# A decode attention kernel: K and V in three pieces per head in place of four, and w_o earlier in the last head

## The chip, the cores and the metric

One core of a Trainium2 chip, the others idle. The metric is the device time of one execution in microseconds. "Span" is what the profile shows between the first and the last instruction; the time is mostly 1.3 to 1.7 us longer, now and then up to 2.9 us, so spans are the steadier number and are given where they decide.

## The reference, cut to what matters

```
x: 1 x 512 (one token), 32 query heads, 8 K/V heads, 65536 cached tokens, head size 128, bf16
q = layernorm(x) @ wq
for each K/V head h:                       # K[h], V[h]: 65536 x 128, 16 MB each
    p = softmax(q[4h:4h+4] @ K[h].T * 128**-0.5)
    o[4h:4h+4] = p @ V[h]
h  = x + o @ wo                            # wo: 4096 x 512, 4 MB
h2 = h + (sigmoid(g) * u) @ w_down         # g, u = layernorm(h) @ w_gate, w_up; 1.75 MB each
```

Nearly everything is the reading of 268 MB of K and V, once.

## The kernel before

SBUF holds a ring of four slots of 32 KB per partition. A load of K or V is 4 MB: 128 rows of 32 KB, 16384 tokens, four loads per head for each of K and V. A slot is split in 8 "chunks" of 4 KB per partition. All loads go through one queue, in order; each waits until its slot is free:

```python
order = [("wq", 0)] + [("K", b) for b in range(NR)]          # NR = 4 loads per head
for b in range(NR, NB):                                       # NB = 32
    order += [("K", b), ("V", b - NR)]
order += [("V", NB - 4), ("V", NB - 3), ("V", NB - 2), ("V", NB - 1), ("wg", 0), ("wu", 0), ("wd", 0)]
# ... slot = position % 4; a load waits for the user of its slot: F{b} (K transposed) or PV{b} (V used)
src = cache[0, h, r * BLK:(r + 1) * BLK, :].rearrange("(p t) d -> p (t d)", t=T)
dma("sp", lambda e, d=dst, sr=src: e.dma_start(d, sr), ..., deps, f"{k}{b}")
if ld == ("V", NB - 4):                                       # w_o follows the last head's first V load
    for i, (j0, nj) in enumerate(WO):                         # WO = ((0, 28), (28, 4)) rows
        dma("sp", ..., f"wo{i}", [f"G{HKV - 1}"] if i == 0 else (), f"wo{i}")
```

DVE transposes K's chunks into a second buffer (8 chunks), PE multiplies them with q (scores), DVE and ACT do the softmax, DVE transposes the probabilities, PE multiplies them with V: "rounds" of 8 matmuls on two chunks of V. The last V load comes in two parts (3 MB and 1 MB). PE's program is one loop over heads with branches for what differs:

```python
if v == NB - 3:                 # last head, after its first V load's rounds
    project7()                  # 28 rows of w_o against the 7 finished heads: one row of 512
...
if v == NB - 1:                 # last head, in front of the last V load's rounds
    columns()                   # that row turned into 4 columns: 4 small fp32 matmuls
op("pe", lambda e: None, [f"V{v}" if v < NB - 1 else f"V{v}.0"] + ...)   # wait for V
pv(v)                           # rounds; before the last one a wait for the last part of V
```

After the last round: output of the head, the last 4 rows of w_o, layernorm, w_gate and w_up, tanh, w_down.

## Time and profile before

| | before |
|---|---|
| time, median of 3 runs | 658.38 us (658.36 to 658.48) |
| span of the profiled run | 657.1 us |
| DMA engines busy | 99.7% of the span |
| PE, DVE busy | 64%, 53% |
| one head's period (eight 4 MB loads) | 77.45 us, 433.2 GB/s |

The prediction below shows the lines. Read them in this order: the engine that is never idle (DMA), then the period of the steady part against its bytes, then who waits at the end. DVE's bracket "[10.27 <-DMA ...]" says that it sat idle for 10.27 us until K arrived: the computing engines follow the stream, they don't lead it.

### The profile page before, as it was taken

The numbers are of one execution on the slowest core, as the hardware profiler recorded it, in microseconds if no ns is written. First come the engines' busy times: TensorE is split into PE (matmuls) and PEld (weight loads), VectorE is DVE, ScalarE is ACT, GpSimd is POOL, SyncE is SP. The second block draws the span as 40 slices with busy tenths as digits, with TensorE's granted clock in tenths as the row PEclk, the third lists the DMA queues.
The fourth block names the chain that finished last, engine by engine and source line by source line (L and its number), as shares of the span: only waits on it lengthen the run. The fifth ranks groups of instructions, "written<-read, shape, count | busy, mean of one in ns | idle before, by whom it ended". The sixth has DMA issues, their size and how long they took to land. (4 is left out here: it accounts for less than half of the span.)

```text
span 657.1 us, 6111 instructions
## 1 busy us (share of the span) xinstructions
PE 420.5 (64%) x2315; PEld 74.1 (11%) x1547; DVE 349.7 (53%) x439; ACT 42.9 (7%) x114; POOL 3.6 (1%) x17
## 2 busy tenths in 40 slices
PE   0688488548666585576765575764866668556746
PEld 0200011011000010010100110101100001001322
DVE  2399775547537665347555374465743575542202
ACT  1100200020000200020000200002000100002001
POOL 1000000000000000000000000000000000000000
PEclk9989689677888697776966769765888869677676
DMA  9999999999999999999999999999999999999998
GB/s 383 447 433 429 439 423 431 431 447 415 447 415 447 437 425 447 415 447 419 443 441 421 447 415 447 423 439 443 419 447 415 447 427 435 445 417 427 435 430 352
DMA packets 10802, 282.34 MB, mean 430 GB/s; under 512 B 1329, under 2 KB 1330, under 8 KB 1842
## 3 DMA queue, kind: packets, MB, share of 16 engines
q1 hardware_dynamic: 10658, 282.33, 99.7%
q10 hardware_dynamic: 144, 0.00, 0.0%
HBM read 282.33 MB, written 0.00 MB: 430 GB/s over the span
## 5 line engine op out<-in xcount | busy, mean ns | idle before, releaser
L431 PE MATMUL PS<-ktw 128*128 128x512 bf16 x1024 | 299.9, 442 | 157.4 <-DVE ktw L511 153.6
L511 DVE STREAM_TRANSPOSE ktw<-ring 128x1024 f32<-128x1024 f32 x256 | 291.6, 1205 | 128.0 <-DMA ring<-in_A_k_cache_dram 128.0
L431 PE MATMUL PS<-ring,PT_sb 128*32 x1024 | 83.9, 455 | 23.6 <-issue 13.2
L431 PEld LDWEIGHTS PS<-ktw 128*128 x256 | 27.1, 106 | 408.2 <-issue 256.8
L565 DVE STREAM_TRANSPOSE PT_sb<-P_sb 128x512 bf16<-128x512 bf16 x32 | 20.2, 684 | 54.0 <-PE PS L602 52.3
L551 ACT ACTIVATE negmax<-PS 128x1 f32<-128x1 f32 x8 | 1.4, 171 | 520.6 <-PE PS L549 520.6
L431 PEld LDWEIGHTS PS<-ring,PT_sb 128*32 x1024 | 25.8, 116 | 79.8 <-issue 74.6
L516 DVE TENSOR_REDUCE M_sb<-PS 128x1 f32<-128x512 f32 x32 | 19.9, 684 | 25.5 <-PE PS L431 25.5
L555 ACT ACTIVATE P_sb<-PS,negmax 128x512 bf16<-128x512 f32 x32 | 21.6, 686 | 0.3
L572 DVE TENSOR_REDUCE lsum<-PS 128x1 f32<-128x4 f32 x8 | 1.3, 163 | 31.2 <-PE PS L570 31.2
L542 PE MATMUL PS<-identf,gm 128*1 128x128 f32 x16 | 3.4, 301 | 16.9 <-DVE gm L540 16.9
L616 DVE TENSOR_TENSOR Lw<-O,blk_of 128x896 bf16<-128x896 bf16 (+1 forms) x2 | 1.4, 683 | 20.6 <-ACT O L606 20.6
L402 PE MATMUL PS<-st,onesf 128*128 128x2 f32 x4 | 1.2, 362 | 16.1 <-DVE st L401 16.1
L431 PE MATMUL PS<-ring,xz 128*8 x32 | 9.2, 459 | 2.3 <-issue 2.3
L599 ACT ACTIVATE po_sb<-PS,rl 128x512 bf16<-128x512 f32 x8 | 5.5, 687 | 53.2 <-PE PS L431 53.2
L431 PE MATMUL PS<-ktw,O 128*1 x26 | 7.6, 464 | 0.0
L549 PE MATMUL PS<-one_f,gmrep 1*128 1x1 f32 x16 | 4.2, 330 | 5.0 <-DVE gmrep L546 5.0
L555 ACT ACTIVATION_READ_ACCUMULATOR P_sb<-PS,negmax 128x1 f32 x32 | 6.5, 202 | 0.0
L476 DVE STREAM_TRANSPOSE qt<-qh 32x512 bf16<-32x512 bf16 x1 | 0.7, 699 | 10.6 <-ACT qh L473 10.6
L602 PE MATMUL PS<-sel_bf,po_sb 128*128 128x4 bf16 x32 | 2.0, 168 | 6.4 <-ACT po_sb L599 6.4
L417 DVE CAST hT<-x_col 128x4 f32<-128x4 bf16 x1 | 0.2, 171 | 10.6 <-DMA x_col<-in_A_x_dram 10.6
L661 DVE COPY yr<-PS 1x512 f32<-1x512 f32 x1 | 0.7, 679 | 8.3 <-PE PS L659 8.3
(82 smaller groups left out, 74.0 us busy)
## 6 DMA issues: line engine op xcount, KB each, us to landing
ring<-in_A_k_cache_dram SPq DMA_DIRECT2D x32, 4096.0 KB, 28.7
ring<-in_A_v_cache_dram SPq DMA_DIRECT2D x31, 4096.0 KB, 26.4
ring<-in_A_wq_dram SPq DMA_DIRECT2D x1, 4096.0 KB, 12.3
ktw<-in_A_wo_dram SPq DMA_DIRECT2D x1, 3584.0 KB, 12.7
ring<-in_A_v_cache_dram SPq DMA_DIRECT2D x1, 3072.0 KB, 13.2
ring<-in_B_w_gate_dram SPq DMA_DIRECT2D x1, 1792.0 KB, 19.0
ring<-in_B_w_up_dram SPq DMA_DIRECT2D x1, 1344.0 KB, 21.7
ring<-in_A_v_cache_dram SPq DMA_DIRECT2D x1, 1024.0 KB, 15.2
```

The source lines that it names most:

```text
L431: return e.add_instruction(mybir.InstMatmult(name=nc.get_next_instruction_name(), engine=mybir.EngineType.PE, ins=[rhs, lhsT], outs=[e.low ...
L511: op("dve", lambda e, d=dst, sr=src: e.transpose(d, sr), deps, f"T{b}.{c}", to="T")
L516: op("dve", lambda e, u=u: e.tensor_reduce(M_sb[:, u % 4:u % 4 + 1], ps(u % NS, 0, 512), AX.X, ALU.max), [f"S{b}.{NC - NR + k}"], f"mx{u}" ...
L542: op("pe", lambda e: e.matmul(ps(MISC, 0, 128, 0, 1), lhsT=gm[:, :], rhs=identf[:, :], start=True, stop=True), [f"gm{h}"], f"gmT{h}", to="Q")
L549: op("pe", lambda e: e.matmul(ps(MISC, 128, 129), lhsT=gmrep[0:1, :], rhs=one_f[0:1, 0:1], start=True, stop=True), [f"gmrep{h}"], f"neg{h}")
L551: op("act", lambda e: e.activation(negmax[:, k:k + 1], ps(MISC, 128, 129), AF.Copy, scale=-att_scale), [f"neg{h}"], f"negmax{h}")
L555: op("act", lambda e, b=b: e.activation(P_sb[:, (b % 4) * 512:(b % 4 + 1) * 512], ps(b % NS, 0, 512), AF.Exp, bias=negmax[:, k:k + 1], sca ...
L565: op("dve", lambda e, b=b: e.transpose(PT_sb[:, (b % 4) * 512:(b % 4 + 1) * 512], P_sb[:, (b % 4) * 512:(b % 4 + 1) * 512]), [f"E{b}", f"o ...
L572: op("dve", lambda e: e.tensor_reduce(lsum[:, :], ps(MISC, 132, 136), AX.X, ALU.add), [f"l{h}"], f"ls{h}", to="D")
L599: op("act", lambda e: e.activation(po_sb[:, :], ps(PO, 0, 512), AF.Copy, scale=rl[:, :]), [f"PV{NR * h + NR - 1}", f"rl{h}"], f"po{h}", to ...
L602: op("pe", lambda e, t=t: e.matmul(ps(OX, 0, 4), lhsT=po_sb[:, t * 128:(t + 1) * 128], rhs=sel_bf[:, 8 * t:8 * t + 8:2], start=(t == 0), s ...
L616: op("dve", lambda e: e.tensor_tensor(Lw[i][:, :].rearrange("p (j c) -> p j c", j=n), bass.AP(tensor=O2, offset=j0, ap=[[NQ, 128], [1, n], ...
```

## The change

Its intent: fewer loads on the stream that bounds the kernel, and work out of the tail. A head's K and V come in pieces of 12, 8 and 12 chunks (48, 32, 48 KB per partition; 6, 4, 6 MB). K and V now overlap in the same ring of 32 chunks, and a piece is freed part by part, by marks in the middle of it. V's rounds are regrouped (10 and 6 in place of 4 x 4). In the last head w_o is loaded between V's first and second piece, and the 28 rows and the columns are done after six rounds. V's last part is 2 MB, two rounds.

```diff
-    SLOT = T * DH
+    PIECES = ((0, 12), (12, 20), (20, 32))
+    RING = 32 * CH
+    AT = {"K": (0, 0, 8), "V": (12, 24, 20), "K0": (0, 12, 20), "V7": (0, 12, 20), "wq": 24, "wg": 0, "wd": 7}
...
+        LAST = [(20, 28), (28, 32)]
...
+        for h in range(1, HKV):
+            load("K", h, 0, ["F0.1" if h == 1 else f"F{h - 1}.3"], "ka", f"K{h}.0")
+            load("V", h - 1, 0, ["F0.3" if h == 1 else f"PV{h - 2}.3:2"], "va", f"V{h - 1}.0")
+            load("V", h - 1, 1, ["F0.4" if h == 1 else f"PV{h - 2}.3"], "vb", f"V{h - 1}.1")
+            load("K", h, 1, [f"F{h}.0"], "ka", f"K{h}.1")
+            load("K", h, 2, [f"F{h}.1", f"PV{h - 1}.0:4"], "kb", f"K{h}.2")
+            load("V", h - 1, 2, [f"PV{h - 1}.0"], "vb", f"V{h - 1}.2")
+        h = HKV - 1
+        load("V", h, 0, [f"F{h}.3"], "va", f"V{h}.0")
+        for i, (j0, nj) in enumerate(WO):
...
+            dma("sp", ..., f"wo{i}", [f"PV{h - 1}.3"] if i == 0 else (), f"wo{i}")
+        load("V", h, 1, (), "vm", f"V{h}.1")
+        for i, cols in enumerate(LAST):
+            load("V", h, 2, (), ("vb", "vl")[i], f"V{h}.2{('', 'b')[i]}", cols)
...
-            op("dve", lambda e: e.memset(scr[:, b:b + 1], 0.0), (), f"F{b}")
+                mark = {7: 0, 11: 1, 23: 3}.get(j, 4 if h == 0 and j == 31 else None)
...
-                for p in ("A0", "B0", "A1", "A2", "A3", "A4"):
+                for p in ("A0", "A4", "B0", "A1", "A2", "A3"):
...
+                    if last:
+                        pv(i - 1, r, 6)
+                    P.part["pe"] = ("L" if last else "V2", i)
+                    if last:
                         project7()
-                        P.part["pe"] = ("VZ", i)
                         columns()
```

F{h}.m are the marks on DVE (after chunk 8, 12, 24 of K), PV{h}.r:n the end of round n of a group on PE.

## The prediction

0.75 us off 658.38 make 657.6, and the 435 GB/s is the fit over packet sizes. That the last two rounds start "about 0.3" after V's landing is an estimate, near the 0.37 us of idle time in front of the last round at 643.26; in front of the rounds before, the same trace has 0.59 (V landed at 632.22, PE starts at 632.81).

> **What bounds the kernel now.** I read the page first (slices, DMA part), then compared the head periods with the bytes that they move, then the DMA queue's own issues, and last the chain that ended the run.
>
> The page's DMA part. The columns of the queue line are packets, MB, share of 16 engines:
>
> ```profile
> DMA  9999999999999999999999999999999999999998
> DMA packets 10802, 282.34 MB, mean 430 GB/s; under 512 B 1329, under 2 KB 1330, under 8 KB 1842
> q1 hardware_dynamic: 10658, 282.33, 99.7%
> ring<-in_A_k_cache_dram SPq DMA_DIRECT2D x32, 4096.0 KB, 28.7
> ring<-in_A_v_cache_dram SPq DMA_DIRECT2D x31, 4096.0 KB, 26.4
> ```
>
> The 16 DMA engines are busy in every slice, 99.7% of the span. PE is busy 64% and DVE 53% of it. The K and V loads take 28.7 and 26.4 us from issue to landing, though one needs only some 9.7 us of the engines: about two others stand before it in the queue when it is issued.
>
> The stretches of one head each (us; busy times of PE, PEld, DVE, ACT, POOL with counts; clock; DMA share; GB/s):
>
> ```profile
> 254.90:332.35 77.45, 48.73 (x266) 7.59 (x170) 42.28 (x51) 4.69 (x13) 0.00 (x0) 0.76 1.00 433
> 487.25:564.70 77.45, 49.85 (x266) 7.47 (x170) 42.29 (x51) 4.69 (x13) 0.00 (x0) 0.79 1.00 433
> ```
>
> The DVE's timeline, arrivals of K:
>
> ```profile
> 486.98 9.13 DVE L511 STREAM_TRANSPOSE ktw<-ring 128x1024 f32<-128x1024 f32 x8 [9.25 <-DMA ring<-in_A_k_cache_dram]
> 506.38 9.13 DVE L511 STREAM_TRANSPOSE ktw<-ring 128x1024 f32<-128x1024 f32 x8 [10.27 <-DMA ring<-in_A_k_cache_dram]
> 564.43 5.75 DVE L511 STREAM_TRANSPOSE ktw<-ring 128x1024 f32<-128x1024 f32 x5 [9.48 <-DMA ring<-in_A_k_cache_dram]
> 583.83 9.13 DVE L511 STREAM_TRANSPOSE ktw<-ring 128x1024 f32<-128x1024 f32 x8 [10.27 <-DMA ring<-in_A_k_cache_dram]
> ```
>
> From 486.98 to 564.43 is 77.45 us for eight loads of 4 MB: 33.554 MB / 77.45 us = 433.2 GB/s, and from 506.38 to 583.83 the same. No gap is left in the stream; DVE waits for it in both places, and a head's compute fits with some 30 us to spare.
>
> The end, from the issue timeline and the chain:
>
> ```profile
> 626.38 0.80 SPq L362 DMA_DIRECT2D ring<-in_A_v_cache_dram  x2
> DMA to landing us min/median/max: 13.2/14.2/15.2
> 628.65 1.38 SPq L354 DMA_DIRECT2D ring<-in_B_w_down_dram  x3
> DMA to landing us min/median/max: 24.4/25.1/25.2
> ...
> 638.08 2.02 PE L667 MATMUL PS<-one_f,yr 1*128 1x1 f32 x8 [1.66 <-issue]
> 640.17 2.72 PE L431 MATMUL PS<-ring,PT_sb 128*32 x24
> 643.26 0.91 PE L431 MATMUL PS<-ring,PT_sb 128*32 x8 [0.37 <-PEq L169]
> 653.58 1.68 PE L831 MATMUL PS<-ring,hhT 128*1 128x128 bf16 x56 [0.98 <-DVE hhT L826]
> ```
>
> The last V load's two parts land at 626.4 + 13.2 = 639.6 and 626.7 + 15.2 = 641.9. But PE is still turning the projected row into columns (638.08 to 640.1, after 1.66 us of issue), so it starts the three rounds late, and the last round only at 643.26, 1.4 us after its data. The last piece of w_down lands at 629.6 + 25.2 = 654.8; the matmuls on it start at 653.58, 30 ns each, and the last 8 would come up at 653.58 + 48 x 0.03 = 655.02. So at the very end compute is the later one, by 0.2 us: the two are balanced.
>
> [...] packets in three stretches (1 us of 32 KB packets, 0.5 us of 14 KB, 0.5 us of 10.5 KB):
>
> ```profile
> q1 hardware_dynamic: 16, 0.52, 121.3%
> q1 hardware_dynamic: 16, 0.23, 107.0%
> q1 hardware_dynamic: 22, 0.24, 111.1%
> ```
>
> One packet is 1.213 x 16 / 16 = 1.213 us; 1.07 x 8 / 16 = 0.535 us; 1.111 x 8 / 22 = 0.404 us. From the first two, (1213 - 535) ns / (32768 - 14336) B = 0.03678 ns per byte, 435 GB/s over 16 engines, and 535 - 14336 x 0.03678 = 7.7 ns per packet; 10752 x 0.03678 + 7.7 = 403 checks it. [...]
>
> **The change part by part.**
>
> *Fewer, larger loads.* Per head 8 loads of 4 MB become 6 (6, 4, 6 MB for K and V each). Bytes are the same. Per engine and head there were 64 data packets of 32 KB and 8 semaphore packets; there will be 48 and 6. At 435 GB/s the bytes of a head take 77.14 us; the measured 77.45 leaves 0.31 us for 72 packets, 4.3 ns each (less than 7.7, because neighbouring packets overlap a little). 18 packets fewer: 18 x 4.3 = 77 ns per head, 8 heads: 0.6 us. If the full 7.7 ns counted, with about as much for a semaphore packet: 18 x 7.7 x 8 = 1.1 us. [...] All of it lies on the bounding stream.
>
> *Buffers.* The ring stays 128 KB per partition. I walked one head with the durations above (a 4 KB chunk, 77.45/64 = 1.21 us of stream; 1.14 us of DVE, 9.13/8; a PE round of two chunks of V 0.9 us), with t = 0 where the head's first K piece begins to move. K's old third piece landed at -14; DVE needs 13.7 us for its 12 chunks and PE about 4 more, so scores end near +4.6. V's old third piece is then used up in six rounds, two by 6.4, all by 10.0. So: next V's first piece can be issued at 6.4, its turn is 14.5; second at 10, turn 29. K's second piece: first K lands about 16, eight transposes to 25, turn 38.7. K's third: 4 transposes and 4 PV rounds later, 35, turn 48.4. V's third: ten rounds done by 44, turn 63. K's next first piece: -8.6, turn 0. The smallest margin is 8 us, so no gap opens. In the start K's second piece of head 1 needs eight transposes behind the softmax of head 0, about 81 (DVE's order puts them ahead of P's transposes now), turn 89. In the last head w_o waits for the old V to be used up, about 602, turn 607: 5 us, the tightest.
>
> *P's transposes and the softmax later.* DVE now transposes the new head's first K block before P, and PE does the softmax after the old V. Both lie beside the stream: 0.
>
> *w_o and its rows earlier.* w_o moves in front of V's second piece. The 28 rows (some 8.2 us in the trace, 615.9 to 624.1) and the columns (2 us, plus the 1.66) then start near 616 and end near 628, with V's second piece landing about 627 and its four rounds done by 632. They leave the tail: PE waits at V's last data instead of arriving 1.4 us late. But that last part is now 2 MB, two rounds, where it was 1 MB, one round.
>
> *The end.* The same bytes follow the last V, so V lands at 641.9 - 0.6 = 641.3. PE starts about 0.3 later, two rounds of 0.9: 643.4, where it was 643.26 + 0.91 = 644.17. The chain up to w_down is unchanged in kind, so its matmuls start 0.75 earlier, at 652.8; w_down's last piece lands at 654.2, and the 48 matmuls before it take until 654.3. Compute and data end together again, about 0.75 us earlier than before. 658.38 - 0.75 = 657.6.
>
> **The rivals.**
> 1. *A new wait.* If the 6 MB pieces come free too late, the stream stops once per head. For it: pieces are bigger, K and V share chunks of the ring, and issue is in order, so one late wait holds all behind it. Against: margins of 5 to 8 us above. A hole of 1 us per head would make 666, with DMA share under 1.00 in the head stretches.
> 2. *The rate doesn't care about packets.* [...] the stream ends at 654.8 as now, the tail may gain only 0.2: 658.2. A 48 KB row cut in two packets would be about 0.3 us worse than now. For it: 4.3 ns is a small remainder of two large numbers. Against: the fit over packet sizes.
> 3. *Projection in the middle as a bound.* If the rows and columns made PE late for V's second and third pieces, the tail would inherit it. For: 12 us of it. Against: about 4 us of idle before V's third piece lands. It would give 658 to 660.
> 4. *The whole packet cost counts.* 1.1 us off: 657.2.
>
> **Range and chances.** Most weight lies on 0.6 us of stream and a tail that keeps up: 657.6. Rivals 2 and 4 make 658.2 and 657.2; runs of the kernel before spread over 0.12 us. So 656.9 to 658.6. Two per cent is 13 us: a gain of that is ruled out by the bytes (282.33 MB at 435 GB/s is 649 us, and start and tail come on top), a loss needs over 1.5 us of hole per head. Chances 0.005, 0.98, 0.015.
>
> **What would show it.** Head period in DVE's arrivals of K: 77.37 (right), 77.45 (rival 2), 77.31 (rival 4), more (rival 1). Packets: about 16 x 144 = 2300 fewer, near 8500. PE idle before the last two rounds, ended by V's last load; columns done near 628. The smallest time from issue to landing of a K or V load not below its own 14.5 us plus a few. The prediction is wrong if DMA share falls under 1.00 in a head, if 48 KB rows appear as more packets, or if the last rounds start long after V's data.

## The result

The changed kernel took 657.96 us in the median of 6 runs (657.93 in that of the five fast ones), the kernel before 658.46 in the same rounds. The ratio is 0.9989, 95% interval 0.9975 to 1.0003: since the interval holds 1, these times alone do not show a gain. What follows rests on spans and traces. A ratio is the mean time of one kernel's fast runs over that of the other's of the same rounds, so not quite the ratio of the medians. One of the six runs took 811.79 us (span 810.4, granted clock 1.0); it counts as slow and is left out. 282 MB in 810 us are 348 GB/s on average; whether the stream was slower throughout or stood still for a time, and why, is open, since no trace of it was kept and it did not come back in 23 more runs of this kernel and its variants.

The page of the changed kernel, its DMA part:

```profile
DMA  9999999999999999999999999999999999999998
DMA packets 8498, 282.33 MB, mean 430 GB/s; under 512 B 1073, under 2 KB 1074, under 8 KB 1586
q1 hardware_dynamic: 8354, 282.33, 99.6%
```

Still no idle slice, and 2304 packets fewer (10802 before). A row of 48 KB is one packet. There are 16 loads fewer, each of 128 rows and, at its end, 16 semaphore packets: 16 x 128 = 2048 data packets and 16 x 16 = 256 semaphore packets are gone (under 512 B: 1329 before, 1073 here).

DVE's arrivals of K's second piece (heads 6 and 7), and the stretch between them:

```profile
486.03 9.13 DVE L496 STREAM_TRANSPOSE ktw<-ring 128x1024 f32<-128x1024 f32 x8 [16.02 <-DMA ring<-in_A_k_cache_dram]
563.41 9.13 DVE L496 STREAM_TRANSPOSE ktw<-ring 128x1024 f32<-128x1024 f32 x8 [15.48 <-DMA ring<-in_A_k_cache_dram]
486.03:563.41 77.38, 53.80 (x266) 7.27 (x170) 42.34 (x50) 4.68 (x13) 0.00 (x0) 0.71 1.00 434
```

The head's period is 77.38 us here, and 464.18 / 6 = 77.36 from 99.23 (the same piece of head 1) to 563.41 (433.7 GB/s), where it was 77.45. The later traces repeat both: 77.36 in e2 and e10 (the changed kernel), 77.45 in e1 (before). In the packets of the trace a 4 MB load takes 9.681 us of stream as before, a 6 MB load 14.500. Half of 4 MB is therefore 14.500 - 9.681 = 4.819 us, so 4 MB without any fixed cost take 9.638, which is 435.2 GB/s, and a load carries 43 ns. Two loads fewer per head are 0.086 us, 0.69 us in eight heads.

The end, on PE's timeline of the changed kernel (in brackets PE's idle time before, and what ended it: PEq is PE's own sequencer, "issue" means that the profile names nothing):

```profile
626.00 2.02 PE L652 MATMUL PS<-one_f,yr 1*128 1x1 f32 x8 [0.77 <-DVE yr L646]
627.96 3.36 PE L415 MATMUL PS<-ring,PT_sb 128*32 x32
636.64 4.49 PE L415 MATMUL PS<-ring,PT_sb 128*32 x32 [5.33 <-PEq L171]
642.14 0.63 PE L415 MATMUL PS<-ring,PT_sb 128*32 x8 [1.00 <-issue]
643.25 0.63 PE L415 MATMUL PS<-ring,PT_sb 128*32 x8 [0.48 <-issue]
653.05 0.99 PE L819 MATMUL PS<-ring,hhT 128*1 128x128 bf16 x56 [1.24 <-DVE hhT L814]
```

The columns are done at 628, as said. But PE is not waiting at V's last part, which landed at 640.9 (issued at 602.6, 38.3 us to landing): its four rounds before run until 641.13, then 1.00 us pass for which the profile names no wait, and the two last rounds end at 643.88, only 0.3 us earlier than before. By the code PE branches to the last wait here; whether that takes the 1.00 us, no run shows. It is not V: in e6 V's last part had landed 8 us before these rounds, and the same place took 1.25 us. And w_down's 56 matmuls took 0.99 us, not 1.68. The granted clock differs with it, in the stretches of before (two) and after (one); the columns are those of the prediction's stretches:

```profile
653.00:654.00 1.00, 0.42 (x20) 0.42 (x24) 0.53 (x1) 0.00 (x0) 0.00 (x0) 0.50 1.01 408
654.00:655.00 1.00, 1.00 (x48) 0.84 (x36) 0.00 (x0) 0.00 (x0) 0.00 (x0) 0.50 0.38 145
```

```profile
653.00:654.00 1.00, 0.95 (x56) 0.76 (x56) 0.00 (x0) 0.00 (x0) 0.00 (x0) 1.00 0.21 80
```

The column after the engines is the clock: 0.50 there, 1.00 here. Yet the clock of these matmuls is not what parts the two spans (657.1 and 656.0): the last packet of w_down's last piece ends at 654.56 before and at 653.40 after, so the stream ended 1.16 us earlier, and each span ends 2.6 us after it. Packets account for 0.69 of this. The rest came by chance: in e2 and e10, the same changed kernel, that packet ends at 653.76 and 653.96, and their streams were already 0.35 and 0.55 us behind this trace when K's second piece of head 1 arrived (99.58 and 99.78 against 99.23). So single profiles can't decide what each part of the change is worth. The experiments go on from there.

### The profile page after: what moved, and what is told of

Its sections match the earlier page's. It is cut to its first block, busy times and chain, and to the rows that moved or that the text cites. A ratio compares the mean times of both kernels' runs of the same rounds, so it can differ in the third digit from the quotient of the medians.

```text
span 656.0 us, 6289 instructions
## 1 busy us (share of the span) xinstructions
PE 439.9 (67%) x2315; PEld 70.0 (11%) x1547; DVE 350.2 (53%) x432; ACT 42.8 (7%) x114; POOL 3.6 (1%) x17
## 2 busy tenths in 40 slices
DMA packets 8498, 282.33 MB, mean 430 GB/s; under 512 B 1073, under 2 KB 1074, under 8 KB 1586
## 5 line engine op out<-in xcount | busy, mean ns | idle before, releaser
L415 PE MATMUL PS<-ktw 128*128 128x512 bf16 x1024 | 293.5, 439 | 103.1 <-DVE ktw L496 96.7
L415 PE MATMUL PS<-ring,PT_sb 128*32 x1024 | 108.3, 517 | 66.5 <-PEq L171 36.7
L415 PEld LDWEIGHTS PS<-ring,PT_sb 128*32 x1024 | 21.7, 116 | 149.1 <-issue 147.4
L531 DVE TENSOR_REDUCE gmj<-PS 1x4 f32<-1x128 f32 x8 | 2.2, 279 | 44.2 <-PE PS L529 44.2
L557 PE MATMUL PS<-L_sb,lsel 128*128 128x4 f32 x16 | 2.5, 229 | 3.8 <-DVE PT_sb L552 3.8
## 6 DMA issues: line engine op xcount, KB each, us to landing
ring<-in_A_v_cache_dram SPq DMA_DIRECT2D x1, 2048.0 KB, 38.3
```

The source lines that it names most:

```text
L415: return e.add_instruction(mybir.InstMatmult(name=nc.get_next_instruction_name(), engine=mybir.EngineType.PE, ins=[rhs, lhsT], outs=[e.low ...
L531: op("dve", lambda e: e.tensor_reduce(gmj[:, :], ps(MISC, 0, 128, 0, 1).rearrange("p (i a c) -> p a i c", a=4, c=NC), AX.XY, ALU.max), [f" ...
L557: op("pe", lambda e: e.matmul(ps(MISC, 132, 136), lhsT=lsel[:, :], rhs=L_sb[:, :], start=True, stop=True), [f"PT{NR * h + NR - 1}"], f"l{h ...
```

## The experiments

Two theories at first. *Stream*: the gain is the fixed cost of the loads that are gone. *Tail*: the gain is the columns taken out of the end. Besides: chance of the clock. Ten runs (the times of all are "same" by the rule of 2%, but e5's, which is "unclear", since its interval lies on both sides of 1.02; so the intervals and spans are read):

| run | time, median us | ratio to before | 95% interval | mean span us | before's, same series |
|---|---|---|---|---|---|
| e1 before again | 659.06 | 1.0009 | 0.9996 to 1.0023 | 657.00 | 657.12 |
| e2 after again | 658.22 | 0.9992 | 0.9979 to 1.0006 | 656.66 | 657.12 |
| e3 quarter rows | 665.48 | 1.0107 | 1.0091 to 1.0122 | 664.20 | 657.12 |
| e4 columns early | 659.77 | 1.0024 | 1.0010 to 1.0037 | 658.38 | 657.12 |
| e5 whole release | 672.95 | 1.0215 | 1.0198 to 1.0232 | 671.05 | 656.97 |
| e6 w_o late | 665.04 | 1.0098 | 1.0081 to 1.0114 | 663.53 | 656.97 |
| e7 columns early, again | 658.98 | 1.0006 | 0.9992 to 1.0020 | 657.70 | 656.91 |
| e8 columns mid | 660.61 | 1.0028 | 1.0015 to 1.0042 | 659.28 | 656.91 |
| e9 w_o's last rows last | 657.57 | 0.9985 | 0.9971 to 0.9999 | 656.28 | 656.91 |
| e10 after, third time | 658.25 | 0.9992 | 0.9978 to 1.0005 | 656.74 | 656.91 |

### e1 and e2: both kernels again

No edit. e1: 

> The kernel before, unchanged, against itself: a null run for the noise and a second trace. Every theory: ratio 1.000, and a period of 19.36 us per two 4 MB loads again. If the last matmuls (w_down) take 1.7 us because of what the kernel does, they do so again; if that was only the clock granted at that moment, their time varies between about 1.0 and 1.7 us from trace to trace.

e2: 

> The changed kernel, unchanged, in more rounds. Stream theory (43 ns saved for each of 16 loads, 0.7 us, by the head periods 77.45 and 77.36 of the two traces): 0.6 to 0.8 us faster, ratio 0.9988 to 0.9991. Clock theory (most of the 1.1 us between the two spans was a luckier clock at the end): under 0.3 us, ratio above 0.9995.

The null run gives 1.0009: a tenth of a per cent is the floor of this timing, and the change is no larger. By the medians e1 was even 0.5 us slower than its twin, though its spans were 0.1 shorter. e2 gives 0.9992, again with 1 in the interval. The spans separate better: 657.00 and 657.12 for before, 656.66 for after, though e2's own five lie between 656.0 and 657.4. w_down's matmuls took 1.97 us in e1's trace and 0.95 in e2's and e10's. The profile gives the time of a single one too (min, median, max, ns; e1, then e2):

```profile
L831 PE MATMUL PS<-ring,hhT x56: 263/311/311, 653.0 to 654.7; 128*1 128x128 bf16 x56
```

```profile
L819 PE MATMUL PS<-ring,hhT x56: 217/219/219, 653.8 to 654.6; 128*1 128x128 bf16 x56
```

The median is 311 in e1 as in the first trace of before, whose clock here was 0.50, and 219 in e2 as in the first of the changed kernel, whose clock was 1.00. That e1 had half the clock and e2 the full one is inferred from that. The kernel does not fix it: e4 and e7 below are one and the same program, and the median is 218 in e4's trace and 311 in e7's. Whether the changed kernel meets the short times more often is open: two runs of before and three of after are too few.

### e3: four times the packets, the same loads

Tells whether the 43 ns belong to the load or to its packets.

```diff
+                    if b < NB - 1:
+                        dst = dst.rearrange("p (a n) -> p a n", a=4)
+                        src = cache[0, h, r * BLK:(r + 1) * BLK, :].rearrange("(a p t) d -> p a (t d)", a=4, p=128)
                     dma("sp", lambda e, d=dst, sr=src: e.dma_start(d, sr), ...)
```

> The kernel before with its loads as they are (same number, 4 MB each), but each row of 32 KB fetched as four runs of 8 KB (K and V permuted alike, so the result stands): 32 data packets per engine and load in place of 8. If the cost goes with the packets (43 ns / 9 packets = 4.8 ns each): 24 x 4.8 = 115 ns more per load, 62 loads, 7 us slower, 665.6, period of two loads 19.59. With the 7.7 ns of the fit over sizes: 185 ns per load, 11.5 us, 670. If it goes with the loads and not with the packets: no change, 658.4, period 19.36.

Measured: 665.48 us, 7 us more. The page's packets and DVE's arrivals of this run:

```profile
DMA packets 34611, 282.35 MB, mean 425 GB/s; under 512 B 1329, under 2 KB 1330, under 8 KB 1842
414.06 9.13 DVE L514 STREAM_TRANSPOSE ktw<-ring 128x1024 f32<-128x1024 f32 x8 [9.38 <-DMA ring<-in_A_k_cache_dram]
492.42 9.13 DVE L514 STREAM_TRANSPOSE ktw<-ring 128x1024 f32<-128x1024 f32 x8 [9.23 <-DMA ring<-in_A_k_cache_dram]
```

A head takes 78.36 us in place of 77.45 with the same eight loads: 0.91 us / (8 x 24 packets) = 4.7 ns per packet and engine. That is the 4.8 that 43 ns / 9 packets gives. So the cost goes with the packets; what is left for a load as such is 43 - 8 x 4.7 = 5 ns, one more packet. This settles the mechanism of the stream theory: what the change saves is packets, by longer rows, and not load instructions. (The shorter rows also lie elsewhere in memory; that two ways give the same 4.7 to 4.8 ns speaks against that as the cause.)

### e5: no release in the middle of a piece

Tests the margin on which the larger pieces live.

```diff
-            load("K", h, 0, ["F0.1" if h == 1 else f"F{h - 1}.3"], "ka", f"K{h}.0")
+            load("K", h, 0, ["F0.1" if h == 1 else f"F{h - 1}.4"], "ka", f"K{h}.0")
-                mark = {7: 0, 11: 1, 23: 3}.get(j, 4 if h == 0 and j == 31 else None)
+                mark = {7: 0, 11: 1, 23: 3}.get(j, 4 if j == 31 else None)
```

> The changed kernel, but a head's first K piece is issued only when the last chunk of the former head's K has been transposed, not the 24th of 32 (one mark moved). The 32nd is transposed about 0.5 to 1 us after the turn of that piece in the stream. If releasing parts of a piece is what keeps the stream whole: a hole of about 2 to 3 us (1 us late plus issue to first byte) for heads 2 to 7, 12 to 18 us in all, 670 to 676, DMA share under 1.00 in the head stretches. If the release time doesn't matter (enough is queued behind): 657.9.

Measured: 672.95 us, about 15 us more than the changed kernel, 2.5 us for each of six heads. One issue, and the stretches around it (DMA share and GB/s are the last two columns):

```profile
287.23 0.33 SPq L324 DMA_DIRECT2D ring<-in_A_k_cache_dram  x1
286.00:287.00 1.00, 1.00 (x7) 0.10 (x1) 1.00 (x2) 0.00 (x0) 0.00 (x0) 1.00 0.01 0
287.00:288.00 1.00, 1.00 (x6) 0.10 (x1) 0.18 (x2) 0.00 (x0) 0.00 (x0) 1.00 0.00 0
288.00:289.00 1.00, 1.00 (x7) 0.13 (x2) 0.00 (x0) 0.00 (x0) 0.00 (x0) 1.00 2.42 737
```

When the load is issued at 287.23, 14 of the 16 engines have run dry; the last packet ends at 287.62, and the first new one starts at 288.18: 0.95 us from the start of the issue to the first packet, in this hole as in four others of this trace. (The first load of before and of the changed kernel, issued at 0.00, shows about the same: first packets at 1.03 and 1.02. The expectation counted 1 to 2 us.) So this one mark, after the 24th of 32 chunks, is what keeps the stream whole in front of K's first piece; the other marks were not moved. (The shares above 1 are packets booked where they start.)

### e6: w_o after V's second piece

```diff
-        for i, (j0, nj) in enumerate(WO):            # w_o
+        load("V", h, 1, [f"PV{h - 1}.3"], "vm", f"V{h}.1")
+        for i, (j0, nj) in enumerate(WO):
...
-        load("V", h, 1, (), "vm", f"V{h}.1")
```

> The changed kernel, but in the last head w_o is loaded after V's second piece instead of before it; the order on PE is kept. The bytes and the end of the stream are the same. w_o lands 9.7 us later (625.6), rows and columns end near 636, V's second piece's rounds near 640.5, the third's near 647.5: PE is 3.5 us behind at the end, so 661 if PE's order in the tail carries the end then. If the stream's end alone counts: 657.9.

Measured: 665.04 us, 7 us more, twice what was expected. PE's timeline:

```profile
637.17 3.34 PE L415 MATMUL PS<-ring,PT_sb 128*32 x32
644.23 4.23 PE L415 MATMUL PS<-ring,PT_sb 128*32 x32 [3.72 <-PEq L171]
```

The rows and columns end at 637.2, a little over the 636 expected. What was not in the estimate is the 3.72 us between the second piece's rounds (done at 640.5) and the third's: the last packets of V's third piece end at 636.0, so PE waits for no data there; by the code it walks its own branches over the parts of the loop that the last head skips. That part of the cause is argued from the code and the releaser (PE's own sequencer); no run took the branches out. In the changed kernel such a walk would cost nothing: PE is idle for 5.33 us before 636.64, and V's third piece landed only at 636.0. So the place of w_o matters: there its rows fill time in which PE waits for V anyway, and leave room for the 3.72 us seen here.

### e4, e7, e8: the columns alone

e4 and e7 are the kernel before with the one part of the change:

```diff
                         project7()
+                        columns()
...
                         P.part["pe"] = ("VZ", i)
-                        columns()
```

> The kernel before with one part of the change alone: the projected row is turned into columns right after the 28 rows instead of in front of the last V load's rounds. PE then starts these rounds at the landing (639.6) and not 0.5 us and more later; the rounds should end some 1 us earlier. Stream theory: the stream still ends at 654.6, so the whole gains 0.3 us at most, ratio above 0.9995. Tail theory (the gain of the change came from the tail): about as fast as the changed kernel, ratio 0.999.

Measured: not faster but slower, spans of 657.0 in the profiled run and 658.2 to 660.1 in the other four. This contradicts the tail theory, and fits the stream theory only in part. Its profile, PE:

```profile
640.17 2.76 PE L431 MATMUL PS<-ring,PT_sb 128*32 x24 [4.21 <-DMA ring<-in_A_v_cache_dram]
```

With the columns gone PE does wait for V here, 4.21 us, and still starts at 640.17, as it did before with the columns in front. V landed at 639.5 (issued at 629.1, 10.4 us), and 0.6 us pass from the landing to the first matmul of the round, here as in e7 (landing 640.0, first matmul 640.60). So in the kernel before the columns ended at the very moment that V could be used: they cost nothing, and there was nothing to gain.

> The kernel with the columns early once more: its timed runs were 1.2 us longer in span than its own profiled one (658.2 to 660.1, against 657.0). Theory: the columns hold up PE by 2 us ahead of the rounds that free the last V load's slot, so this load is issued at 629.1 and not at 626.4, 2 us before its turn (631.1); with 0.95 us from issue to the first packet (seen in the run with the whole release) a PE that is 1 us slower opens a hole. Then the runs are again 1 us or so longer, and a profile that fell on such a run shows the first packets of this load after the last of its predecessor. Rival: it was that series' noise; then 658.5 as the kernel before.

The excess came back, smaller: spans of 657.2 to 658.4, mean 0.8 us over before. In this profile the last V load was issued at 630.12 (626.38 before, 629.12 in e4):

```profile
630.12 0.80 SPq L362 DMA_DIRECT2D ring<-in_A_v_cache_dram  x2
640.60 2.76 PE L431 MATMUL PS<-ring,PT_sb 128*32 x24 [4.37 <-DMA ring<-in_A_v_cache_dram]
```

From the end of its predecessor's packets to the end of its first part's, the load took 7.27 us in the traces of both runs of before, 7.48 in e4 and 7.79 in e7: 0.2 and 0.5 us more, growing with the later issue. It is hardly a hole: in e4 no engine stood idle, and in e7 three of 16 did for a moment. What grew are the load's first packets, up to 1.32 us each in e4 and 1.58 in e7, where all of them take 0.91 in before, e1 and e8. So the theory's 0.95 us to the first packet is not what was paid, as e4's load was issued 2 us before its turn; a cost that comes with the late issue is seen in these two traces, why the packets take longer is not shown. That the unprofiled runs with 1 to 3 us more paid the same, only more, is not shown either, as they left no trace.

e8 was to keep the columns early without the late release, by moving rows and columns one part on:

```diff
-                    if v == NB - 3:
+                    if v == NB - 2:
-            away("br_eq", w, w0 - 4, "rows_of_o", lambda: section("L"))
+            away("br_eq", w, w0 - 8, "rows_of_o", lambda: section("L"))
```

> The kernel before with the rows and the columns one part later, after the rounds that free the last V load's slot, while PE waits for V's third load anyway. The columns have left the tail and nothing is released later. Late-release theory: the extra 1.2 us is gone, spans of 656.9 to 657.2 as the kernel before. Tail theory (columns out of the tail are worth something by themselves): spans at 656.5 or less. If early columns as such cost 1.2 us, spans stay at 658.3.

None of the three expectations held: spans of 659.28, 2.4 us over before. The load was issued early again (626.7), but there are 10 us of rows and columns, and only about 6 us of waiting in that place:

```profile
635.28 2.02 PE L667 MATMUL PS<-one_f,yr 1*128 1x1 f32 x8 [0.77 <-DVE yr L661]
642.64 2.68 PE L431 MATMUL PS<-ring,PT_sb 128*32 x24 [2.88 <-issue]
```

PE starts V's last rounds at 642.64 and not at 640.17, 2.5 us late, and the whole is 2.4 us late. The 2.88 us in front of them are no wait for V, whose part had landed at 639.7; the profile names nothing there, and what they are is not shown. As a test of the late release it failed, by its design. What it does show: this lateness of PE at the end is paid nearly one for one, so the tail has little slack on PE's side.

### e9 and e10: give PE room at the end

That suggested a version to beat both. The last 4 rows of w_o are needed only after the last head's output, so they can follow V, and V lands 1.2 us earlier with the same end of the stream.

```diff
-        for i, (j0, nj) in enumerate(WO): ...          # both parts of w_o here
+        load_wo(0)
         load("V", h, 1, (), "vm", f"V{h}.1")
         for i, cols in enumerate(LAST):
             load("V", h, 2, (), ("vb", "vl")[i], f"V{h}.2{('', 'b')[i]}", cols)
+        load_wo(1)
```

> The changed kernel, but the last 4 rows of w_o (0.5 MB, 1.2 us of stream), needed only after the last head's output, are loaded after V's last piece and not before its second. V lands 1.2 us earlier, the stream ends as before. In the changed kernel PE's last matmuls begin 0.0 to 0.6 us after w_down's last piece could have been used, so up to that is gained: spans of 656.0 to 656.3 against 656.5 of the changed kernel, 657.7. If the stream's end alone sets the time: 656.4 to 656.5, no gain.

e10 is the changed kernel in the same series: 

> The changed kernel in the same series as the run with w_o's last rows after V, for comparison: spans 656.0 to 656.7, mean 656.5; ratio 0.999.

e9's mean span is 656.28, e10's 656.74, before's 656.91; e9's ratio to before is 0.9985, the only interval of a faster version that stays under 1, and only just (0.9999). The spans of e9 (656.1 to 656.5) and e10 (656.5 to 656.9) touch but do not overlap. PE at the end, e10 and then e9:

```profile
654.01 0.95 PE L819 MATMUL PS<-ring,hhT 128*1 128x128 bf16 x56 [0.97 <-DVE hhT L814]
```

```profile
652.43 0.62 PE L822 MATMUL PS<-ring,hhT 128*1 128x128 bf16 x32 [0.98 <-DVE hhT L817]
653.33 0.40 PE L822 MATMUL PS<-ring,hhT 128*1 128x128 bf16 x16 [0.28 <-DMA ring<-in_B_w_down_dram]
653.96 0.28 PE L822 MATMUL PS<-ring,hhT 128*1 128x128 bf16 x8 [0.23 <-DMA ring<-in_B_w_down_dram]
```

In e10 PE comes to w_down at 654.01 and waits for none of it (the last piece, issued at 618.5, landed within 35.8 us, by 654.3; the last 8 matmuls come up at 654.8): PE sets the end. In e9 PE comes at 652.43 and waits twice for w_down: the stream sets the end. That is where part of the expected gain of the change had gone, and the packets show it directly. w_down's last packet ends at 654.56 and 654.28 in the two traces of before, at 653.40, 653.76 and 653.96 in the three of the changed kernel: on average 654.42 and 653.71, 0.71 us earlier, where 0.69 was counted. The span ends 2.56 us after it in both of before and 2.53 in e9, but 2.57, 2.95 and 2.93 in the changed kernel: in two of its three traces PE's tail lost 0.4 us of the gain.

## Why the prediction was right, point by point

- *The bound and the fixed cost of a packet.* Right. Predicted 4.3 ns per packet, head period 77.37, 0.6 us in all; measured 77.36, 4.8 from the two load sizes and 4.7 from e3, 0.69 us. (With the 435.2 GB/s of the two load sizes in place of the rounded 435, the prediction's own sum gives 4.8.) That it is less than the 7.7 of the fit "because neighbouring packets overlap a little" agrees with the records: eight packets of 1.213 us alone are 9.70 us, and the whole load takes 9.681. Rivals 2 (no cost per packet) and 4 (all 7.7 ns) are out.
- *Packets.* "Near 8500": 8498. 48 KB rows were not cut. (The "about 0.3 us worse" for cut rows was mis-summed: 14 packets more per engine and head x 4.3 ns x 8 heads are 0.5 us.)
- *Buffers.* Right within a microsecond, but for V's first piece, 2.3 us early. Head 7's first K piece begins to move at 514.2 in the trace. Issues counted from there, predicted and measured: its own -8.6, -9.0; V's first 6.4, 4.1; V's second 10, 9.4; K's second 25, 24.5; K's third 35, 35.6; V's third 44, 44.4. w_o: about 602, 600.8. No hole; rival 1 fails here, and e5 shows what it would have cost. That a late wait holds the loads behind it is seen at the end: w_gate, which by the code waits only for the transposes of a K load that begin at 564.43 in before, is issued at 627.22, 629.96 and 630.97 in before, e4 and e7, each time 0.84 to 0.85 us after V's last load (626.38, 629.12, 630.12). One step of the walk was too simple: it counts a load as free of cost as long as it is issued before its turn. No trace had shown that, and e7's load, issued 1.3 us before the first engine was free for it, took 0.5 us longer. The margins of 5 us and more hid this.
- *Rows and columns.* "Near 616 to near 628, rounds done by 632": 616.6, 628.0, 631.3. Rival 3 does not occur in that place.
- *The end.* The sum stayed in the range, but its terms were mis-sized, and this is the weakest part. "PE starts about 0.3 later, two rounds of 0.9: 643.4": PE starts a round 0.6 us after a landing (0.59 in before, 0.6 in e4 and e7), V's four rounds before took 1.1 us each, not 0.9, and 1.00 us passed between them and the last two; so 642.14 and 643.88. And "the matmuls on it start at 653.58, 30 ns each" took what one trace shows at a clock of 0.50 for the cost of a matmul: at 1.00 it is 0.99 us / 56 = 18 ns. "They leave the tail: PE waits at V's last data instead of arriving 1.4 us late" was wrong: the columns had cost nothing (e4), and PE arrives at V's last data 1.2 us after its landing still. With this, two of the prediction's own signs went against it: PE's idle time before the last two rounds was not ended by V's last load, and these rounds did start well after V's data.
- *The time.* 657.6 predicted, 657.96 measured, 658.22 and 658.25 in the repeats, all inside the range of 656.9 to 658.6. This tests little, since the range holds the 658.38 of the kernel before too, that is, no change at all; it is the head's period and the end of the stream that bear the prediction out. Of the 0.75 us foreseen, the spans of the series with both kernels show 0.46 (e2) and 0.17 (e10): the stream's 0.7 less what PE's tail did not follow.

## What to carry to other kernels

When the DMA stream never stops, compare the period of the steady part with its bytes over the rate that two sizes of load give (435.2 GB/s here): what was left, 0.35 us of 77.45, was the fixed cost of packets, and longer rows (not fewer load instructions) lowered it. It is small: 0.1% of a head's time between rows of 32 and 48 KB (77.45 and 77.36 us), 1.2% between 8 and 32 KB (78.36 in e3). The larger pieces were safe here because they are freed in parts, early enough before their turn (e5); count that margin from issue to turn, and keep it well above the time to the first packet (0.95 us in e5; with 1.3 us ahead of the first free engine, e7's load still lost 0.5). Where stream and compute finish together, as here, look whether the other side has room for a gain on one (PE's tail lost 0.4 us of it in two of three traces): order what is loaded last by when it is needed.
